# Expert stage of a routed kernel: weight loads coded per layer, one three-way branch per half of a unit, register loads in a unit's middle, the last scatter behind the late work

## The chip, the cores and the metric

The kernel runs on one core of one Trainium2 chip. The metric is the device time of one execution in microseconds (us), lower is better. The core has five engines with one instruction queue each: TensorE (PE; PEld is its weight load), VectorE (DVE), ScalarE (ACT), GpSimd (POOL) and SyncE (SP), which here issues the loads from HBM. A q behind an engine's name means its sequencer, which reads registers, takes branches and waits on semaphores.

## The reference, cut to what matters

An attention step and a dense layer are computed first. What the change touches is the third part, a mixture of experts over 2304 tokens of width 512, 8 experts, hidden width 1024:

```
expert_idx = np.argmax(logits, axis=1)
gate_w = probs[np.arange(N), expert_idx]
for e in range(E):
    mask = expert_idx == e
    h = np.maximum(x[mask] @ w1[e], 0.0)
    out[mask] = gate_w[mask, None] * (h @ w2[e])
```

w1[e] is 512x1024 and w2[e] is 1024x512, both in float32 (2 MB each).

## The kernel before, in words

The tokens are sorted by expert on the chip and cut into units of 256 places. A unit holds tokens of one expert. How many units there are, which expert each has and whether its second 128 places are filled is known only at run time, so it stands in an integer tile, `ctl` (row 0 the expert, row 1 a mode for the weights, row 2 the kind), and the engines read it into registers. In these data units U0 to U12 have work. Kind 2 is a double unit (both halves of 128), kind 0 a thin one (64 tokens at most, laid out so that the high and low parts share a matmul). Double are U0, U1, U2, U5, U6, U7, U10, U12; thin are U3, U4, U8, U9, U11.

A float32 product is made of three matmuls: high times high, high times low, low times high (`mm3`, L109 to L111). So weights are split after loading: ACT rounds a 128x1024 piece to a high part (L77), DVE subtracts for the low part (L78). There are two sets of split weights, one for even and one for odd units, and one staging set (tiles `sg`, `sq`, `sr` for w1, `sd`, `se` for w2). A unit needs new weights only where its expert differs from that of two units before: U3, U5, U6, U9, U10, U11.

The work stands in an order written by hand (`manual_schedule`), unit after unit. `gather` (POOL, L1016) fetches the rows of unit U+2; `group` makes the hidden values of a double unit, `grouped` their relu and split; `xt_turns` transposes the rows of the next unit, `xt_split` splits them, `fill` splits its weights from staging; `down` makes the output, `scale` (DVE) applies the gate and `scatter` (POOL, L1123) writes the rows out. A thin unit does the same in `single`, with its weights as the moving operand (L1141), 64 columns folded back by a matmul with `dots` (L1184). Where kind 1 would need the third product, a branch (L1145) takes either that product or as many matmuls with a zero tile `wz` (L1150, L1057).

For SP, `fetch(U)` stands behind unit U. It has three branches (L988), for units U+2, U+3 and U+4; the mode says which of them loads all of a unit's 4 MB (`fetch_all`: four DMAs of 512 KB for w1, L930, and four for w2, L933, each of these behind one of w1). The first DMA waits until staging is free, that is, until the last split of the earlier weights. `early_split` splits the weights of U0 and U1, which come in 256 KB pieces (`es`), ahead of this. `plan()` makes the tables: `counted`, `chain`, `placed` (the row lists, tile `perm`) and `listed` (`ctl`). Code for four further units (LATE, L1482) stands behind U12 and is jumped over.

Of the kernel before, what the change touches and what calls it, by code (L numbers as in the profile page):

```python
# [42 lines left out]
LATE = [range(U1, U1 + 2), range(U1 + 2, NU)]  # L43
SCALE = 1.0 / math.sqrt(D)
# [6 lines left out]
SOON = 400  # L51


def body(tc, x, state, w_in, w_out, ee, tau, w1, w2, out):
# [58 lines left out]
    with stack:  # L113
# [69 lines left out]
        def norm(ss, y, r, act=True):  # L183

            tsc(ss, ss, 1e-30, ALU.max)
            if act:
                A.activation(y, ss, AF.Ln)
                A.activation(y, y, AF.Exp, scale=0.5)
            else:
                G.tensor_tensor(out=y, in0=ss, in1=mb_[:, 3:4].to_broadcast(list(ss.shape)), op=ALU.pow)  # L190
            V.reciprocal(r, y)
# [435 lines left out]
        def route_n(c):  # L627
# [4 lines left out]
            norm(ssq[:, t0 : t0 + n], y, r, False)  # L632
# [62 lines left out]
        ctl = rt.tile([P, 3, NU], I32, name="ctl")  # L695
# [114 lines left out]
        def plan():  # L810
# [12 lines left out]
            def chain():  # L823
# [32 lines left out]
                oq = cut(NT, NX)  # L856
# [8 lines left out]
            def listed():  # L865
                cs, cx = held["cs"], held["cx"]
                kk, kb, gk, new = cut(NL), cut(NL), cut(NL), cut2(NU)
                V.memset(new[:, 0:U0], 1.0)
                c1, c2, c3 = (cut2(NL, NE) for _ in range(3))
# [13 lines left out]
                tsc(kk, new[:, 1 : NU - 1], 0.0, ALU.is_equal, -1.0, ALU.mult)  # L883
                tsc(gk, new[:, 0 : NU - 2], 0.0, ALU.is_equal, 1.0, ALU.add)
                tt(gk, gk, kk, ALU.mult)
                stt(ctl[:, 1, U0:NU], gk, 3.0, new[:, U0:NU], ALU.add, ALU.mult)
                tsc(ctl[:, 2, 0:1], n, float(U0), ALU.add)

                one, two = cut(NE), cut(NE)
# [8 lines left out]
                V.tensor_copy(ctl[:, 2, U0:NU], kk)  # L898

            return counted, chain, placed, listed  # L900
# [15 lines left out]
        staged, flag, mode = {}, {}, {}  # L916
        xg, gt_, xo, xth, xtl, hth, htl, hq, y_, ix_, ys_, hs_ = ({} for _ in range(12))
        FENG = [ET.Activation, ET.DVE]

# [9 lines left out]
        def fetch_all(e):  # L929
            one = [Y.dma_start(staged[1, i], w1[bass.ds(e, 1), i * P : (i + 1) * P, :].rearrange("o p f -> (o p) f")) for i in range(4)]  # L930
# [580 lines left out]
```

## Time and profile before

| | |
|---|---|
| median of 3 runs | 737.47 us (736.97 to 737.89) |
| the profiled execution | 734.5 us, its span 732.7 us |
| busy over the span | PE 93%, PEld 79%, DVE 65%, ACT 60%, POOL 25% |
| mean granted TensorE clock | 0.967 of full speed |
| expert stage (U0's first group to the end) | 425.36 to 732.7 us |

PE is busy for most of the span, so what can be won in the stage lies where its busy time is below the stretch's length, where its clock is below 1, or in work that needn't be there. The stage is cut at the starts of the units for this.

### The profile page before, as it was taken

The numbers are of one execution on the slowest core, as the hardware profiler recorded it, in microseconds if no ns is written. First come the engines' busy times: TensorE is split into PE (matmuls) and PEld (weight loads), VectorE is DVE, ScalarE is ACT, GpSimd is POOL, SyncE is SP. The second block draws the span as 40 slices with busy tenths as digits, with TensorE's granted clock in tenths as the row PEclk, the third lists the DMA queues.
The fourth block names the chain that finished last, engine by engine and source line by source line (L and its number), as shares of the span: only waits on it lengthen the run. The fifth ranks groups of instructions, "written<-read, shape, count | busy, mean of one in ns | idle before, by whom it ended". The sixth has DMA issues, their size and how long they took to land. (4 is left out here: it accounts for less than half of the span.)

```text
span 732.7 us, 12086 instructions
## 1 busy us (share of the span) xinstructions
PE 681.2 (93%) x3913; PEld 579.2 (79%) x3913; DVE 477.9 (65%) x1025; ACT 437.9 (60%) x771; POOL 183.7 (25%) x163
## 2 busy tenths in 40 slices
PE   8898999989999999999999999899888999859894
PEld 8898867768888888888878788888676997749593
DVE  5987898897587866766698778836273524543630
ACT  5877989988697768667867763225264212441510
POOL 2785356641000200300141420301310222101101
PEclk9899999999999999999999999999999999969898
DMA  8552243430010544411224452562834631427000
GB/s 200 152 154 87 59 144 114 144 116 0 1 58 14 143 104 100 93 40 58 73 58 138 151 173 58 174 234 86 294 109 188 236 112 61 164 100 263 32 2 33
DMA packets 58253, 82.84 MB, mean 113 GB/s; under 512 B 25051, under 2 KB 35803, under 8 KB 58149
## 3 DMA queue, kind: packets, MB, share of 16 engines
q1 hardware_dynamic: 54388, 70.31, 31.8%
q0 software_dynamic: 3760, 11.30, 4.6%
q8 instruction: 46, 0.75, 0.4%
q14 instruction: 59, 0.48, 0.2%
HBM read 65.32 MB, written 13.65 MB: 108 GB/s over the span
## 5 line engine op out<-in xcount | busy, mean ns | idle before, releaser
L109 PE MATMUL acc<-woh,gh 128*128 128x512 f32 x272 | 109.0, 404 | 4.9 <-ACT gh L77 4.9
L110 PE MATMUL acc<-wol,gh 128*128 128x512 f32 x272 | 107.7, 397 | 0.0
L111 PE MATMUL acc<-woh,gl 128*128 128x512 f32 x272 | 94.8, 402 | 0.5 <-DVE gl L78 0.5
L109 PE MATMUL hp<-xth,w1h 128*128 128x256 f32 x256 | 76.3, 298 | 9.8 <-ACT w1h L77 8.5
L111 PE MATMUL hp<-xth,w1l 128*128 128x256 f32 x256 | 76.5, 299 | 5.9 <-DVE w1l L78 5.3
L110 PE MATMUL hp<-xtl,w1h 128*128 128x256 f32 x256 | 75.0, 293 | 0.6 <-DVE xtl L78 0.6
L1123 POOL DMA_INDIRECT out<-ys,ix x21 | 21.6, 1029 | 212.3 <-DVE ix L1126 116.0
L109 PEld LDWEIGHTS acc<-woh,gh 128*128 128x128 f32 x272 | 51.2, 188 | 18.0 <-ACT gh L77 8.0
L111 PEld LDWEIGHTS acc<-woh,gl 128*128 128x128 f32 x272 | 51.2, 190 | 14.2 <-DVE gl L78 3.1
L518 ACT ACTIVATE er<-h,mb__104 128x512 f32<-128x512 f32 x68 | 46.6, 685 | 26.0 <-PE h L111 23.8
L109 PEld LDWEIGHTS hp<-xth,w1h 128*128 128x128 f32 x256 | 51.1, 200 | 11.3 <-ACT w1h L77 9.5
L110 PEld LDWEIGHTS acc<-wol,gh 128*128 128x128 f32 x272 | 51.4, 189 | 10.1
L1109 ACT ACTIVATE hth<-hp 128x512 fp32r<-128x512 f32 (+1 forms) x34 | 17.8, 532 | 67.5 <-PE hp L111 56.3
L111 PEld LDWEIGHTS hp<-xth,w1l 128*128 128x128 f32 x256 | 51.1, 199 | 8.6 <-DVE w1l L78 7.9
L524 DVE TENSOR_TENSOR er<-er 128x512 f32<-128x512 f32 x56 | 40.0, 715 | 21.6 <-ACT er L518 21.1
L547 ACT ACTIVATE h<-er,mb__104 128x512 f32<-128x512 f32 x68 | 47.3, 696 | 9.2 <-DVE er L524 5.6
L110 PEld LDWEIGHTS hp<-xtl,w1h 128*128 128x128 f32 x256 | 51.2, 200 | 1.1 <-DVE xtl L78 0.8
L109 PE MATMUL h<-xh,mh 128*128 128x512 f32 x128 | 51.6, 403 | 0.3 <-ACT xh L77 0.3
L110 PE MATMUL h<-xl,mh 128*128 128x512 f32 x128 | 50.7, 396 | 0.4 <-DVE xl L78 0.4
L111 PE MATMUL h<-xh,ml 128*128 128x512 f32 x128 | 50.6, 396 | 0.0
L548 ACT ACTIVATE er<-er,mb__104 128x512 f32<-128x512 f32 x68 | 49.4, 726 | 1.4
L519 ACT ACTIVATE u<-h 128x512 f32<-128x512 f32 x68 | 40.4, 594 | 0.0
(475 smaller groups left out, 1728.8 us busy)
## 6 DMA issues: line engine op xcount, KB each, us to landing
w<-in_moe_w_in SPq DMA_DIRECT2D x16, 512.0 KB
w<-in_moe_w_out SPq DMA_DIRECT2D x16, 512.0 KB
es<-in_moe_w SPq DMA_DIRECT2D x32, 256.0 KB
sg<-in_moe_w SPq DMA_DIRECT2D x12, 512.0 KB
sd<-in_moe_w SPq DMA_DIRECT2D x12, 512.0 KB
se<-in_moe_w SPq DMA_DIRECT2D x12, 512.0 KB
xn<-in_x SPq DMA_DIRECT2D x32, 128.0 KB
md<-mr SPq DMA_DIRECT2D x28, 128.0 KB
```

Of the source, the lines that this page charges most:

```text
L109: T.matmul(o, lh, rh, start=first, stop=False)
L110: T.matmul(o, lh, rl, start=False, stop=False)
L111: T.matmul(o, ll, rh, start=False, stop=last)
L518: A.activation(z, h, AF.Tanh, scale=0.5, bias=mb_[:, 0:1])
L519: A.activation(u, h, AF.Silu)
L524: V.tensor_tensor(out=z, in0=z, in1=z, op=ALU.mult)
L547: A.activation(r, z, AF.Square, scale=QS, bias=mb_[:, 1:2])
L548: behind["ACT"] = A.activation(z, z, AF.Square, scale=QS, bias=mb_[:, 2:3])
L1109: A.activation(hi, i, AF.Relu)
L1123: G.indirect_dma_start(out=out[:, :], out_offset=bass.IndirectOffsetOnAxis(ap=ix_[U][r], axis=0), in_=ys_[U][r], in_offset=None, bounds_ch ...
```

## The change

`plan()` makes one more table, `plan_` (in the unused part of `dots`): for each place behind a unit the expert whose w1 is to be loaded there, the one whose w2 is, or 8 for none, and for each unit a code `due_` of what is to be split in it. `listed` is cut into `experts`, `shapes` and `codes` and stands between the groups of U1. `fetch(U)` has two branches in place of three, and each loads one layer (`fetch_part`). With these data U3's weights are loaded behind U0, U5's behind U2, U6's w1 behind U3 and its w2 behind U4, U9's behind U5, U10's w1 behind U7 and its w2 behind U8, U11's behind U9. `fill(U)` splits what the next unit needs, `fill_soon(U)` the w1 of the unit after the next: U5's in U3 and U9's in U7, with only their w2 left for U4 and U8.

`either`, with its branches on `kp` and `kf` inside `single`, becomes `chosen`, a branch with three ways, taken once for the upper half of a unit (`up`) and once for the lower (`out_of`). Between the halves stands `next_rows`: the splits, and the register loads for units further on (`AHEAD`). The zero matmuls are gone, and both halves of the next rows are always transposed. Around U1 some pieces of `early_split` go to other places and four of them to POOL, U1's first group goes ahead of `placed`, and U1's `down` alternates between its two outputs. The scatter of U12's second half, from tiles of its own (`ixe`, `yse`), stands behind the LATE code.

```diff
+        def fetch_part(e, part):
             for i in range(4):
-                src = w2[bass.ds(e, 1), 2 * i * P : 2 * (i + 1) * P, :].rearrange("o (t p) d -> p (o t) d", p=P)
-                two = Y.dma_start(staged[2, i].rearrange("p (t d) -> p t d", t=2), src)
-                tc.add_manual_dep(two.ins, one[i].ins.name, mybir.DependencyInfo(mybir.DependencyClass.Sync, mybir.DependencyReason.DATA), reason="first layer first")
+                if part == 1:
+                    Y.dma_start(staged[1, i], w1[bass.ds(e, 1), i * P : (i + 1) * P, :].rearrange("o p f -> (o p) f"))
+                else:
+                    src = w2[bass.ds(e, 1), 2 * i * P : 2 * (i + 1) * P, :].rearrange("o (t p) d -> p (o t) d", p=P)
+                    Y.dma_start(staged[2, i].rearrange("p (t d) -> p t d", t=2), src)
...
-            for ahead in (1, 2, 3):
-                u = U + 1 + ahead
-                if u < U1:
-                    if u not in first:
-                        first[u] = expert(u, [ET.SP])
-                        mode[u] = nc.values_load(ctl[0:1, 1, u : u + 1], engines=[ET.SP], min_val=0, max_val=3)
-                    with tc.If(mode[u] == 4 - ahead):
-                        fetch_all(first[u])
+            for part in (1, 2):
+                cell = plan_[0:1, part, U : U + 1]
+                code = nc.values_load(cell, engines=[ET.SP], min_val=0, max_val=NE)
+                with tc.If(code < NE):
+                    fetch_part(nc.values_load(cell, engines=[ET.SP], min_val=0, max_val=NE - 1), part)
 
         def fill(U):
 
-            if U in flag:
-                with tc.If(flag[U] > 0):
-                    with tc.If(flag[U] > 1):
-                        split_all(U, [1])
-                    split_all(U, [2])
-            if U + 1 in flag and U > U0:
-                with tc.If(flag[U + 1] == 1):
+            with tc.If(due_[U] > 1):
+                with tc.If(due_[U] > 2):
                     split_all(U + 1, [1])
...
+                split_all(U + 1, [2])
+
+        def fill_soon(U):
+
+            with tc.If(due_[U] == 1):
+                split_all(U + 2, [1])
...
         def kinds(U):
 
-            for u in (U, U + 1):
-                if u < U1 and u not in flag:
-                    flag[u] = nc.values_load(ctl[0:1, 1, u : u + 1], engines=FENG, min_val=0, max_val=3)
-            kind[U], kp[U], kf[U] = (nc.values_load(ctl[0:1, 2, U : U + 1], engines=e, min_val=0, max_val=2) for e in ([ET.PE, ET.Pool] + FENG, [ET.PE], FENG))
+            cell = ctl[0:1, 1, U : U + 1]
+            kf[U] = nc.values_load(cell, engines=FENG, min_val=0, max_val=2)
+            kind[U] = nc.values_load(cell, engines=UENG, min_val=0, max_val=2)
+
+        def dues(U):
+            if U < END:
+                due_[U] = nc.values_load(plan_[0:1, 0, U : U + 1], engines=FENG, min_val=0, max_val=3)
...
         def xt_turns(U, parts=range(2)):
-            for i in parts:
-                for k in range(2 * i, 2 * i + 2):
-                    T.transpose(wide2(xo[U][i])[:, k % 2, 0:P], xg[U][0][:, k * P : (k + 1) * P], ident)
...
-            def second():
+            for r in range(2):
                 for i in parts:
                     for k in range(2 * i, 2 * i + 2):
-                        T.transpose(wide2(xo[U][i])[:, k % 2, P : 2 * P], xg[U][1][:, k * P : (k + 1) * P], ident)
...
-            with tc.If(kp[U] > 1) as w:
-                second()
-            with w.Else():
-                for k in range(2 * len(parts)):
-                    T.matmul(xo[U][1][:, 511:512], wz, wz[:, 0:1], start=True, stop=True, skip_group_check=True)
+                        T.transpose(wide2(xo[U][i])[:, k % 2, r * P : (r + 1) * P], xg[U][r][:, k * P : (k + 1) * P], ident)
...
-                with tc.If(kf[U] > 1) as w:
+                with tc.If(kf[U] > 0) as w:
...
+        def ends(U):
             ix_[U] = [rt.tile([P, 1], I32, tag="ix", bufs=2, name=f"ix{U}{r}") for r in range(2)]
             ys_[U] = [cv.tile([P, DM], F32, tag="cx", bufs=2, name=f"ys{U}{r}") for r in range(2)]
...
+            if U == END:
+                ix_[U][1] = rt.tile([P, 1], I32, name="ixe")
+                ys_[U][1] = ep.tile([P, DM + 2], F32, tag="xg", bufs=2, name="yse")[:, 0:DM]
...
-                scatter(U, r)
+                if U != END or not r:
+                    scatter(U, r)
...
+        def chosen(U, do):
+
+            with tc.If(kind[U] > 1) as w:
+                do(U, 2)
             with w.Else():
...
+                with tc.If(kind[U] > 0) as v:
+                    do(U, 1)
+                with v.Else():
+                    do(U, 0)
+
+        def up(U, n):
+            def rows_of_next():
+                if U + 1 in xo:
+                    xt_turns(U + 1)
+
+            if n > 1:
+                for j in range(4):
+                    group(U, j)
+                    grouped(U, j)
+                rows_of_next()
+                return
...
-
-            def turns(m):
-                with tc.If(kp[U] > 0) as w:
-                    for k in range(4):
-                        T.transpose(tr[m][:, k * P : (k + 1) * P], h[m][:, k * P : (k + 1) * P], ident)
...
-            if U + 1 < U1:
-                xt_turns(U + 1)
+            rows_of_next()
             turns(1)
             turned_(1)
-            following_rows(U)
...
+        def out_of(U, n):
+            if n > 1:
+                down(U)
+                store(U)
+                return
...
+        def next_rows(U):
+
+            if U < END:
+                xt_split(U + 1)
+                fill(U)
+            for u in AHEAD.get(U, ([], []))[0]:
+                kinds(u)
+            for u in AHEAD.get(U, ([], []))[1]:
+                dues(u)
+            if U + 2 <= END:
+                fill_soon(U)
...
-            early_split(2, V, G)
+            early_split(2, V)
...
+            early_split(2, V)
...
             group(0, 1)
+            early_split(3, V)
             squares(LC)
-            early_split(len(jobs) - 16, V, G)
...
-            early_split(2, V)
-            given = route_n(LC)
+            given = route_n(LC, lambda: early_split(3, V))
...
             grouped(0, 3)
+            xt_split(1)
+            early_split(4, G)
...
             down(0, [0], range(2, NFE))
-            down(0, [1], range(6))
+            down(0, [1])
+            ends(0)
+            for r in range(2):
+                scale(0, r)
+            rooms(1)
+            group(1, 0)
             placed()
             gather(2)
+            for r in range(2):
...
             tt(fold, ident[:, 0:HP], ident[:, HP:P], ALU.add)
-            down(0, [1], range(6, NFE))
-            store(0)
-            listed()
-            early_split(4, V)
-            rooms(1)
-            for j in range(4):
-                group(1, j)
-                grouped(1, j)
-                early_split(2, V)
...
+            grouped(1, 0)
+            group(1, 1)
+            experts()
+            grouped(1, 1)
+            early_split(2, V)
+            group(1, 2)
+            grouped(1, 2)
+            shapes()
+            group(1, 3)
+            grouped(1, 3)
+            codes()
             es_stack.close()
...
             stages()
             fetch(0)
-            for U in range(1, U1):
-                if U + 1 < U1:
-                    kinds(U + 1)
+            gather(3)
+            xt_tiles(2)
+            xt_turns(2)
+            kinds(2)
+            dues(1)
+            next_rows(1)
+            ends(1)
+            down(1, [(r, k) for k in range(NFE) for r in range(2)], None)
+            store(1)
+            fetch(1)
...
                 with cond(U):
-                    if U + 1 < U1:
+                    if U < END:
                         xt_tiles(U + 1)
-                    if U > 1:
-                        rooms(U)
-                    gather(U + 2)
-                    if U > 1:
-                        either(U)
+                    rooms(U)
+                    if U + 2 <= END:
+                        gather(U + 2)
+                    chosen(U, up)
+                    next_rows(U)
+                    if U < END:
+                        ends(U)
                     else:
-                        xt_turns(U + 1)
-                        following_rows(U)
-                        down(U)
-                        store(U)
-                fetch(U)
-
-            more = ExitStack()
+                        V.tensor_copy(ix_[U][1], gt_[U][1][:, 1:2])
+                    chosen(U, out_of)
+                if U + 2 <= END:
+                    fetch(U)
...
-                    either(U)
-            more.close()
+                    chosen(U, up)
+                    ends(U)
+                    chosen(U, out_of)
+            late.close()
+            scatter(END, 1)
```

On SP, the loads behind one unit. Before, this is the last of the three branches behind a unit (L988) with the reads for the next (L942 the expert, L987 the mode):

```order
L933 ISA
L933 DMA sd_5336<-in_moe_w 128x2x512
L933 ISA
L933 DMA se_5334<-in_moe_w 128x2x512
L933 ISA
L933 DMA se_5337<-in_moe_w 128x2x512
L988 UNCONDITIONAL_BRANCH x2
L942 TENSOR_LOAD ctl
L942 ISA x2
L987 TENSOR_LOAD ctl
L987 ISA x2
L988 COMPARE_AND_BRANCH
```

After, the two branches (L1026) for a layer each; a register is read from `plan_` (in `dots`) ahead of the branch and again inside it:

```order
L975 DMA se_5350<-in_moe_w 128x2x512
L1026 UNCONDITIONAL_BRANCH x2
L1025 TENSOR_LOAD dots
L1025 ISA x2
L1181 UNCONDITIONAL_BRANCH
L1091 UNCONDITIONAL_BRANCH
L1031 UNCONDITIONAL_BRANCH
L1038 UNCONDITIONAL_BRANCH
L1026 COMPARE_AND_BRANCH
L1027 TENSOR_LOAD dots
L1027 ISA x2
L972 ISA
```

The w1 DMAs (L972) and the w2 DMAs (L975) now stand in branches of their own, so one can be issued behind one unit and the other behind a later one, and no expert is read outside of the branch.

On PE, the middle of a thin unit. Before (L1057 is the last of the zero matmuls for the next rows, L1179 the branch on the kind, L1141 the output's matmuls):

```order
L1057 MATMUL gt_5697<-wz 128x1
L1057 LDWEIGHTS wz
L1057 MATMUL gt_5697<-wz 128x1
L1053 UNCONDITIONAL_BRANCH
L1187 UNCONDITIONAL_BRANCH
L1179 COMPARE_AND_BRANCH
L1181 MATMUL hp_5700<-ident,hs_5716 128x128 x4
L1179 UNCONDITIONAL_BRANCH
L1184 MATMUL hp_5700<-dots,hs_5716 128x64 x4
L1179 UNCONDITIONAL_BRANCH
L1141 MATMUL y_5703<-w2h_4601,hth_5705 128x512 x2
L1141 MATMUL y_5703<-w2h_4658,hth_5705 128x512 x2
```

After, the same place (L1081 the transposes of the next rows, L1212 the folding matmul, L1059 the register loads, L1181 the branch for the lower half):

```order
L1081 MATMUL gt_5648<-ident,xg_5404 128x128 x2
L1212 MATMUL hp_5651<-dots,hs_5663 128x64 x4
L1184 UNCONDITIONAL_BRANCH
L1059 TENSOR_LOAD ctl
L1059 ISA x2
L1059 TENSOR_LOAD ctl
L1059 ISA x2
L1091 UNCONDITIONAL_BRANCH
L1031 UNCONDITIONAL_BRANCH
L1038 UNCONDITIONAL_BRANCH
L1026 UNCONDITIONAL_BRANCH
L1181 COMPARE_AND_BRANCH
```

The branch ahead of the folding matmul is gone; behind it there are now the end of the three-way branch, the register loads, which stood at the unit's head before, and a new branch, whose thin side is reached by a jump over the double side and that of kind 1.

On POOL, the end. Before (L1123 the scatters of the last unit's second way, L1217 the end of its branch, L1482 the LATE branches):

```order
L1145 UNCONDITIONAL_BRANCH
L1210 UNCONDITIONAL_BRANCH
L1123 DMA out<-ys_12492,ix_12490 2176x512
L1217 ISA
L1217 UNCONDITIONAL_BRANCH
L1482 ISA
L1482 UNCONDITIONAL_BRANCH
L1482 ISA
L1482 UNCONDITIONAL_BRANCH
L1507 ISA
```

After (L1147 the scatters, L1546 the LATE branches):

```order
L1184 UNCONDITIONAL_BRANCH
L1147 DMA out<-ys_12311,ix_12309 2176x512
L1181 ISA
L1184 UNCONDITIONAL_BRANCH
L1546 ISA
L1546 UNCONDITIONAL_BRANCH
L1546 ISA
L1546 UNCONDITIONAL_BRANCH
L1147 DMA out<-yse,ixe 2176x512
L1572 UNCONDITIONAL_BRANCH
L1572 ISA
```

The last scatter, from `yse`, is now behind all the branches and behind the two ISA rows of L1546, which count POOL's DMA queue on.

## Rows read from the trace of the kernel before

**Rows 1.** By unit: length, PE, PEld, DVE, ACT, POOL busy, PEclk, DMA, GB/s
```profile
459.34:475.29 15.95, 14.00 (x98) 13.22 (x96) 12.62 (x43) 3.71 (x7) 6.95 (x6) 0.89 0.57 183
...
487.92:511.25 23.33, 23.33 (x153) 21.15 (x152) 11.99 (x16) 10.42 (x14) 2.97 (x3) 1.00 0.50 170
511.25:522.35 11.10, 10.91 (x74) 8.63 (x72) 4.46 (x14) 2.26 (x6) 1.02 (x1) 1.00 0.76 266
522.35:536.07 13.72, 11.63 (x73) 8.79 (x73) 4.99 (x10) 5.78 (x10) 6.39 (x6) 1.00 0.65 218
536.07:563.36 27.29, 25.37 (x158) 21.90 (x155) 13.70 (x19) 10.54 (x15) 2.93 (x3) 1.00 0.50 179
563.36:592.60 29.24, 25.94 (x153) 22.94 (x152) 15.68 (x23) 9.82 (x13) 5.00 (x5) 0.94 0.53 191
592.60:617.64 25.04, 23.47 (x153) 20.98 (x152) 10.22 (x17) 6.63 (x10) 4.50 (x5) 1.00 0.16 45
617.64:629.32 11.68, 10.96 (x72) 8.70 (x73) 4.12 (x9) 5.99 (x10) 2.46 (x3) 1.00 0.23 72
629.32:652.01 22.69, 12.70 (x72) 10.31 (x72) 6.80 (x12) 5.64 (x11) 2.94 (x3) 0.81 0.62 212
652.01:679.99 27.98, 27.89 (x153) 24.85 (x153) 14.35 (x21) 11.31 (x16) 2.94 (x3) 0.85 0.48 173
679.99:698.96 18.97, 15.46 (x74) 11.27 (x72) 11.77 (x18) 8.06 (x12) 2.02 (x2) 0.82 0.09 31
...
721.87:732.70 10.83, 0.01 (x1) 0.00 (x0) 0.75 (x1) 0.00 (x0) 0.98 (x1) 0.67 0.09 29
```

**Rows 2.** What PE waited for, 487 to 722: total, times, longest
```profile
PE hp L109 <- ACT w1h L77: 8.5, 1, 8.5
```

**Rows 3.** The same for SP's queue, and for ACT's splits, 480 to 733
```profile
SPq L930 <- DVEq L999: 69.0, 5, 34.0
...
ACT w1h L77 <- SPq L988: 28.5, 5, 9.6
```

**Rows 4.** SP's DMA issues, U10's weights: start, us, line, op
```profile
631.51 1.06 SPq L930 DMA_DIRECT2D sg<-in_moe_w  x2
...
638.26 2.27 SPq L933 DMA_DIRECT2D se<-in_moe_w  x2
```

**Rows 5.** PE in order of time, places in U4, U8 and U9
```profile
530.40 0.66 PE L1048 MATMUL gt<-ident,xg 128*128 128x128 f32 x4
...
628.36 0.35 PE L1150 MATMUL y<-wz 128*128 128x1 bf16 x8
...
652.01 0.58 PE L109 MATMUL hp<-xth,w1h 128*128 128x256 f32 x1 [8.45 <-ACT w1h L77]
```

**Rows 6.** PE's sequencer, branches of a line: ns min/median/max, first and last start
```profile
L1217 PEldq COMPARE_BRANCH  x19: 65/287/4006, 485.2 to 717.6; - x19
...
L1217 PEldq COMPARE_BRANCH  x1: 1052/1052/1052, 521.0 to 521.0; - x1
...
L1179 PEldq COMPARE_BRANCH  x10: 207/210/4690, 511.7 to 691.2; - x10
```

**Rows 7.** Splits and a small operation around U1, 400 to 480
```profile
L78 DVE TENSOR_TENSOR w2l<-es,w2h x11: 681/692/1685, 420.0 to 479.1; 128x512 fp32r<-128x512 f32 x11
...
L78 POOL TENSOR_TENSOR w2l<-es,w2h x4: 1286/1306/1610, 419.5 to 435.5; 128x512 fp32r<-128x512 f32 x4
...
463.43 0.23 DVE L64 TENSOR_SCALAR ph<-iof,ph 128x16 f32<-128x16 f32 x1
```

**Rows 8.** ACT and DVE in order of time, U5's first split of w1
```profile
533.72 2.01 ACT L77 ACTIVATE w1h<-sg 128x1024 fp32r<-128x1024 f32 x2 [0.30 <-SPq L988]
...
534.81 2.36 DVE L78 TENSOR_TENSOR w1l<-sg,w1h 128x1024 fp32r<-128x1024 f32 x2 [0.42 <-ACT w1h L77]
```

**Rows 9.** The end: POOL's last scatter, and its queue at the LATE branches
```profile
723.48 0.98 POOL L1123 DMA_INDIRECT out<-ys,ix  x1 [5.13 <-DMA out<-ys,ix]
...
L1482 POOLq INC_SWDGE_SEM  x1: 1105/1105/1105, 726.8 to 726.8; - x1
```

More of the change, by code (lines that the diff above doesn't have):

```diff
@@ L855, in chain @@
                 stt(g, g, 2.0, second, ALU.mult, ALU.add)
-                oq = cut(NT, NX)
+                oq = held["oq"] = cut(NT, NX)
                 tt(oq, row(iof[:, 0:NX], NT), col(g, NX), ALU.is_equal)
@@ L882, in listed, with shapes @@
                 tt(new[:, U0:NU], kk, gk, ALU.mult)
[L883 to L889, printed above, removed]
+                tsc(ctl[:, 1, 0:1], n, float(U0), ALU.add)
+            def shapes():
+                cs, one, two = held["cs"], cut(NE), cut(NE)
                 for w, blank in ((one, P), (two, P + P // 2)):
@@ L1131, in store, with high @@
                 scale(U, r)
-                scatter(U, r)
+                if U != END or not r:
+                    scatter(U, r)
         def lanes(t, half):
             return t.rearrange("p (k t) -> p k t", t=P)[:, :, half * HP : (half + 1) * HP]
-        def high(o, terms):
+        def high(o, terms, last):
             n = len(terms)
@@ L1140, in high, with low, sums @@
                 for k, (h, _, *w) in enumerate(terms):
[L1141 to L1143 removed]
+                    T.matmul(o, h, w[low], start=not low and k == 0, stop=last and bool(low) and k == n - 1)
+        def low(o, terms):
             n = len(terms)
[L1145 to L1167 removed]
+            for k, (_, l, wh, _) in enumerate(terms):
+                T.matmul(o, l, wh, start=False, stop=k == n - 1)
+        def sums(o, terms, thick):
+            high(o, terms, not thick)
+            if thick:
+                low(o, terms)
+        def chosen(U, do):
+            with tc.If(kind[U] > 1) as w:
+                do(U, 2)
+            with w.Else():
+                with tc.If(kind[U] > 0) as v:
[12 more added lines that the diff above has]
+                return
             q = U % 2
@@ L1214, in single, with cond @@
             scatter(U, 0)
-        def either(U):
-            with tc.If(kind[U] > 1) as w:
-                double(U)
-            with w.Else():
-                single(U)
+        def next_rows(U):
[8 more added lines that the diff above has]
+                fill_soon(U)
+        def cond(U):
+            return nullcontext() if U < UMIN else tc.If(nblk > U)
         steps = [(c, f) for c, a, b in RUNS for f in range(a, b)]
@@ L1425, in body @@
             places_of(range(CHUNKS[LC][0], NT))
-            counted, chain, placed, listed = plan()
+            counted, chain, placed, experts, shapes, codes = plan()
             down(0, [0], range(2))
@@ L1454, in body @@
+            kinds(2)
[5 more added lines that the diff above has]
+            fetch(1)
+            for U in range(2, U1):
+                if U == END:
+                    ends(U)
+                    V.memset(ix_[U][1], 2 * NTOK)
+                    V.memset(ys_[U][1], 0.0)
                 with cond(U):
-                    if U + 1 < U1:
+                    if U < END:
@@ L1472, in body @@
                 for U in g:
-                    gather(U, late=True)
+                    gather(U)
                     kinds(U)
-                    fetch_all(expert(U, [ET.SP]))
+                    e = expert(U, [ET.SP])
+                    for part in (1, 2):
+                        fetch_part(e, part)
                     split_all(U)
```

152 lines of the change are left out of this document (76 added, 76 removed).

## The prediction

> **What bounds the kernel now.** I read first the table of units [rows 1]: a unit's length against PE's busy time and PE's clock. U2 shows a double unit with nothing in its way: 23.33 us, PE busy for all of it, clock 1.00. U3 shows a thin one: 11.10 us. Held against these, the losses stand in a few rows: U5 is 27.29, U6 29.24, U7 25.04 and U10 27.98 against 23.3; U4 is 13.72, U9 22.69 and U11 18.97 against 11.1. Together these are 4.0 + 5.9 + 1.7 + 4.7 + 2.6 + 11.6 + 7.9 = 38.4 us, part idle PE, part PE at a lower clock (0.81 to 0.85 in U9 to U11). U1 has 1.95 us idle and a clock of 0.89.
>
> Then what PE waited for: one wait of 8.5 us, ahead of U10's first matmul, on ACT's split of its w1 [rows 2, 5]. Next, who was late for ACT: SP's branch, 28.5 us in 5 splits, 9.6 the longest [rows 3]. SP's branch is passed only when all eight loads have landed. And what was SP late for: it waited 69.0 us in 5 fetches for DVE's last split to free the staging, 34.0 us in one of them [rows 3]. So in U5 to U11 weights set the pace: one staging set, filled in one go and freed in one go. For U10 the loads were issued from 631.51, the last two at 638.26 to 640.53 [rows 4]; since a w2 load is issued only behind the landing of a w1 load, a layer takes about 640.5 − 631.5 = 9 us at most, two about 17, an estimate.
>
> The slow clock follows the idle time: U9's stretch, whose last 8.45 us are idle, has 0.81, and U10's busy time is 27.89 for the work that takes 23.33 in U2 [rows 1, 5].
>
> **The change, part by part.** The sum is made against the profiled execution: span 732.7, time 734.5 us, which is 3.0 below the median 737.47. The result is given at the median, so 3.0 is added at the end.
>
> *Loads per layer.* w1's staging is now free when w1 is split, and the new w1 can land while w2's staging is still full. U9's w1 is loaded behind U5 and split in U7, so U10's w1 can be asked for behind U7, not in the middle of U9. At U9's start (in the old times 629) it has had all of U8, 11.7 us, against the 9 of a layer: it has landed. Splitting it falls into U9's second half, as U5's did into U4's: there the split began at 533.72 and U5 began at 536.07 [rows 1, 8], which cost U5 27.29 − 23.33 = 4.0. I take this for U10: 27.3, so −0.7. U9 loses its wait and runs at full clock: 11.25, −11.4 (8.45 is the wait [rows 5], the rest clock and one late split). U11 then starts after an unbroken stretch: 11.4, −7.6. U5's w1 is split in U3, so U5 falls to 23.7, −3.6. U6 has its weights behind U3 and U4, with all of U5 for the split: 23.7, −5.5. U7, 25.04 with 23.47 busy: 24.3, −0.7. U8: 11.4, −0.3.
>
> Against this, U5's w1 split now stands on ACT and DVE around U4's start. Four pieces take about 4.2 us on ACT (2.01 for two) and 4.7 on DVE (2.36 for two) [rows 8], and U4's relu and split wait behind them in the queues, PE for these. Below, nothing (the pieces are done before U4 begins); above, the whole 4.7. U4's old stall was 13.72 − 11.63 = 2.1 [rows 1], and I take 14.5, +0.8.
>
> *Zero matmuls and transposes.* The eight behind a thin unit's output go (0.35 us in U8 [rows 5]), and two or three groups of four (half as many each); four transposes come wherever the next unit is thin, 0.66 us from the first start to the last end by U4's row [rows 5]; since matmuls overlap I take 0.4. U2 becomes 23.7 (+0.4). For thin units the two nearly cancel; U3 is set to 11.8 (+0.7), for the register loads now in its middle. If no engine's other work covers them there, they cost about 1 us in each of U3, U4 and U8; bounds 0 to 3 in all.
>
> *Around U1.* U1's idle 1.95 us goes if its w1 pieces are split earlier; part of its clock loss (15.95 × 0.11 = 1.75) with it. I take −2.4 from at most −3.7. The other bound is dearer: four pieces go to POOL, ahead of `chain`. A piece takes POOL 1.31 us, and DVE's like piece takes 0.69 us at the median but 1.69 at worst [rows 7]. Four times 1.31 = 5.2 us is what `chain`, and so U2's rows, can be later, which makes this term −2.4 to +2.8. [...] `codes` is about 21 small DVE operations at 0.23 [rows 7], 4.8 us behind U1's last group. U1's `down` covers them (24 matmuls for each half stand behind), and U3's weights, due only in U2's second half, cover SP's later start. Without the cover they'd cost the 4.8.
>
> *The last scatter.* Before, POOL's queue waited 5.13 us for the scatter before it, ended with that, issued at 723.48, 1.6 after PE's end at 721.87, and then counted its queue on for 1.1 us [rows 1, 9]. After, that count stands ahead of the scatter, hidden by U12's `down`. −1.0, between 0 and −1.6.
>
> *The sum.* Units: +0.4 +0.7 +0.8 −3.6 −5.5 −0.7 −0.3 −11.4 −0.7 −7.6 = −27.9. U1 −2.4, the end −1.0. New idle gaps (U4, U10) can pull the clock down again as in U9; for this +2, an estimate between none and the 4.6 that U10 paid. Together −29.3: the profiled execution would go to 705.2, the median to 708.2; I say **708.5 us**.
>
> **Rivals.**
>
> *Jumps (a).* Each thin unit now takes two long jumps on PE's sequencer, over the double side of each half, where it took one. The long branch of before (L1217) took 1.05 us at U4, 4.01 at its worst; its median over all units is 0.29, and the short branch L1179 took 0.21 at the median and 4.69 once [rows 6]. Why a branch takes 0.2 or 4 the rows don't tell. If the second jump stands on the path in all five thin units, this adds 5 × 1.05 to 5 × 4.01 = 5 to 20, middle 12.6, so about 721. For it speaks that nothing is queued on PE between the halves but the output, which waits for ACT and DVE anyway; against it, that this wait covers the cheap jumps, and that the halves are shorter than the whole that is jumped over now. Chance 0.17. [...]
>
> *Slower (b).* The same jumps with one more in each half: kind 0 is reached over the body of kind 2 and over that of kind 1. That is four taken branches in a thin unit, of which one was paid before. Two more exposed at the dear price, (4.01 + 4.69) / 2 = 4.35, on five units give 43.5, so 752. It ends above 737.5 from 29 / 5 = 5.8 us of new exposed branch time in each thin unit. The rows against it: of L1179's ten, the median is 0.21. Chance 0.05.
>
> *The loads come no earlier (c).* A layer's loads are still issued by one queue, and a branch not taken still waits for what landed before. If U10's w1 is held up so that it lands when it did, U9, U10 and U11 keep their length: 19.7 of the 29.3 are gone, 727.5. For it speaks the 34 us wait, which shows how one late split shifts everything; against it, that U9's w1 is split two units ahead. Chance 0.07.
>
> *More (d).* U4 and U10 have no stall, the clock stays up, U1's idle time and its clock loss go whole: −1.5, −4, −2, −1.3 and some of U7's 1: 699. Chance 0.07 for less than 699.
>
> **How the numbers follow.** The main case, 699 to 714 (U1's term alone reaches +5.2), has 0.64. Below 699 lie 0.07, between 714 and 724 (a) for the most part, above 724 the rest of (a), (c) and (b), about 0.15. The range is 697 to 724. A measurement of this kernel can tell about 0.2%, 1.5 us: only (b) and a part of what I don't see end above 739, so faster 0.93, same 0.01, slower 0.06.
>
> **What would show it.** In the profile after: no wait of PE for ACT of more than 4 us behind U4; U9 and U11 near 11.4 us at a clock near 1; SP's longest wait for DVE well under 34; U10's w1 issued about a unit earlier than U9's middle; U4 with a stall on ACT or DVE of 2 to 3 us. Wrong would be branches of PE's sequencer of over 2 us ahead of the lower halves with PE idle behind them (a, b), a PE wait ahead of U10 as before (c), or U2's start later than 487.9, which is where U1's part would have failed.

## The result, and the profile after

The changed kernel takes **704.29 us** (median of 4 runs, 698.74 to 705.4) against 737.22 in the runs beside it: ratio 0.955, 95% interval 0.9487 to 0.9614, or 33 us less. The forecast was 708.5, range 697 to 724. Six later runs gave 703.09 (700.22 to 707.35). The profiled execution, 698.74 us with a span of 696.9, is the fastest of its four, so its rows flatter the change: span against span it is 35.8 us, of which some 3 are not the usual case (U1 and the clock, below).

First the table of units again, of the changed kernel (length, then busy time of PE, PEld, DVE, ACT, POOL, then PE's clock, DMA share and GB/s). The first row is U1 up to its output, then come U2 to U11, and the end:

```profile
458.40:473.88 15.48, 13.02 (x122) 12.74 (x121) 14.72 (x52) 3.43 (x6) 6.42 (x6) 1.00 0.27 76
...
485.19:508.77 23.58, 23.58 (x154) 21.23 (x153) 13.48 (x20) 10.31 (x14) 4.00 (x4) 1.00 0.46 146
508.77:521.28 12.51, 10.45 (x58) 8.40 (x56) 4.80 (x12) 5.31 (x10) 4.45 (x4) 1.00 0.87 314
521.28:534.69 13.41, 10.54 (x56) 8.64 (x57) 7.71 (x14) 6.77 (x11) 3.11 (x4) 1.00 0.83 305
534.69:558.33 23.64, 23.64 (x154) 21.45 (x153) 18.10 (x22) 13.11 (x17) 2.94 (x3) 1.00 0.35 118
558.33:581.77 23.44, 23.44 (x153) 21.29 (x152) 6.60 (x15) 3.48 (x6) 5.00 (x5) 1.00 0.66 238
581.77:605.24 23.47, 23.47 (x154) 21.30 (x152) 9.47 (x16) 6.79 (x10) 4.01 (x4) 1.00 0.36 102
605.24:617.76 12.52, 10.47 (x58) 8.38 (x56) 5.18 (x10) 6.21 (x10) 2.98 (x3) 1.00 0.43 137
617.76:628.88 11.12, 10.68 (x57) 8.59 (x57) 6.97 (x13) 6.05 (x10) 2.95 (x3) 1.00 0.69 234
628.88:655.08 26.20, 24.51 (x153) 21.41 (x152) 21.50 (x26) 16.19 (x21) 2.95 (x3) 1.00 0.52 186
655.08:665.45 10.37, 10.33 (x57) 8.59 (x57) 3.97 (x11) 2.94 (x6) 2.01 (x2) 1.00 0.16 56
...
688.53:696.90 8.37, 0.00 (x1) 0.00 (x0) 0.75 (x1) 0.00 (x0) 0.98 (x1) 0.67 0.10 36
```

Against [rows 1], U5, U6 and U7 are now as long as PE is busy in them, with a clock of 1.00; U9 has gone from 22.69 to 11.12 and U11 from 18.97 to 10.37. U10 is the one double unit with a loss left, U3, U4 and U8 the thin ones. What PE and ACT still wait for, from U1 and from U2 on:

```profile
PE y L111 <- DVE ph L71: 2.5, 1, 2.5
PE hp L1167 <- issue: 2.4, 2, 1.4
PE hp L1167 <- ACT w1h L79: 2.0, 1, 2.0
...
PE hp L113 <- DVE w1l L80: 1.0, 2, 0.5
...
ACT w2h L79 <- SPq L1026: 0.6, 2, 0.3
```

The wait of 8.5 us [rows 2] has no successor, and of ACT's 28.5 us for SP's branch [rows 3] 0.6 are left. SP itself still waits for staging, in more and smaller pieces, and asks for U10's w1 in U7 (before, in U9 [rows 4]):

```profile
SPq L972 <- DVEq L1038: 44.3, 3, 18.1
...
SPq L972 <- DVE w1l L80: 22.7, 5, 21.0
```

```profile
598.69 1.47 SPq L972 DMA_DIRECT2D sg<-in_moe_w  x2
```

The clock differs from run to run (0.98 to 0.99 over the span). In the profile shown it never falls in the units; in a second profile of the same kernel (run again below, span 700.2) U1 and U4 read

```profile
459.70:488.70 29.00, 25.98 (x171) 23.09 (x170) 20.18 (x75) 4.51 (x8) 6.46 (x6) 0.94 0.43 126
524.90:538.20 13.30, 12.02 (x56) 9.79 (x57) 7.53 (x14) 6.58 (x11) 2.96 (x4) 0.87 0.84 302
```

which is a granted clock of 0.94 and 0.87 of full speed over the two, where PE was idle for 3.0 us in U1 and for 2.1 us right ahead of U4. U1 takes 29.0 us there for 26.8 in the profile shown. Another 2.9 us between the two profiles lie ahead of U0, in work that the change doesn't touch, where the clock is lower as well (0.95 and 0.98 in the first two stretches of 100 us, against 0.97 and 1.00).

### The profile page after: what moved, and what is told of

Its sections match the earlier page's. It is cut to its first block, busy times and chain, and to the rows that moved or that the text cites. A ratio compares the mean times of both kernels' runs of the same rounds, so it can differ in the third digit from the quotient of the medians.

```text
span 696.9 us, 11870 instructions
## 1 busy us (share of the span) xinstructions
PE 661.4 (95%) x3833; PEld 566.1 (81%) x3833; DVE 482.6 (69%) x1042; ACT 438.6 (63%) x771; POOL 184.4 (26%) x165
## 4 chain that ended last, share of the span: by engine, by line
PE 36%; DMA 27%; issue 12%; DVE 11%; ACT 9%; POOL 2%; SPq 2%; POOLq 0%; DVEq 0%; ACTq 0%
DMA out<-ys,ix 18%; PE acc L113 6%; PE acc L111 6%; PE acc L112 6%; DMA xg<-x1d,perm 4%; PE h L111 3%; PE h L112 3%; PE h L113 3%; DMA w<-in_moe_w_out 2%; SPq L329 2%; PE lg L628 2%; DMA w<-in_moe_w_in 1%; DMA es<-in_moe_w 1%; ACT er L522 1%; ACT h L551 1%
## 5 line engine op out<-in xcount | busy, mean ns | idle before, releaser
L113 PE MATMUL hp<-xth,w1l 128*128 128x256 f32 x256 | 72.5, 283 | 1.2 <-DVE w1l L80 1.0
L111 PE MATMUL hp<-xth,w1h 128*128 128x256 f32 x256 | 72.4, 283 | 0.5 <-DVE htl L74 0.5
L112 PE MATMUL hp<-xtl,w1h 128*128 128x256 f32 x256 | 72.2, 282 | 0.6 <-DVE xtl L80 0.6
L1147 POOL DMA_INDIRECT out<-ys,ix x20 | 20.2, 1008 | 171.7 <-DVE ix L1151 75.0
L113 PEld LDWEIGHTS hp<-xth,w1l 128*128 128x128 f32 x256 | 48.2, 188 | 1.8 <-DVE w1l L80 1.8
L111 PEld LDWEIGHTS hp<-xth,w1h 128*128 128x128 f32 x256 | 48.2, 188 | 1.2 <-DVE htl L74 0.7
L112 PEld LDWEIGHTS hp<-xtl,w1h 128*128 128x128 f32 x256 | 48.2, 188 | 1.2 <-DVE xtl L80 0.8
L111 PE MATMUL y<-w2h,hth 128*128 128x512 f32 x96 | 38.8, 404 | 2.6 <-DVE ph L71 2.5
```

Of the source, the lines that this page charges most:

```text
L111: T.matmul(o, lh, rh, start=first, stop=False)
L112: T.matmul(o, lh, rl, start=False, stop=False)
L113: T.matmul(o, ll, rh, start=False, stop=last)
L1147: G.indirect_dma_start(out=out[:, :], out_offset=bass.IndirectOffsetOnAxis(ap=ix_[U][r], axis=0), in_=ys_[U][r], in_offset=None, bounds_ch ...
```

## The experiments

Each was timed in 5 rounds. Ratios are to the kernel before; 0.01 is 7.4 us.

| run | what | median us | ratio (95%) |
|---|---|---|---|
| again | the change | 703.09 | 0.9578 (0.954 to 0.9616) |
| regs_head | register loads at the head | 703.65 | 0.9589 (0.9551 to 0.9626) |
| whole | that, and one branch for a unit | 716.78 | 0.9769 (0.9731 to 0.9807) |
| pad_up | code never run, in what is jumped over | 734.17 | 0.9972 (0.9942 to 1.0001) |
| joint | both layers loaded and split together | 711.94 | 0.9700 (0.9661 to 0.9739) |
| one_if | that, in one branch | 709.47 | 0.9627 (0.9586 to 0.9667) |
| idle_if | that, with a branch never taken behind | 725.16 | 0.9861 (0.9824 to 0.9898) |
| undo_all | whole and idle_if together | 739.57 | 1.0064 (1.004 to 1.0088) |
| last_back | last scatter in its old place | 704.76 | 0.9553 (0.951 to 0.9596) |
| split_v | four pieces on DVE, not POOL | 701.59 | 0.9546 (0.9526 to 0.9567) |
| shapes_early | table of kinds one group earlier | 699.55 | 0.9486 (0.9444 to 0.9528) |
| thin_first | that, with the thin way first | 706.33 | 0.9597 (0.9582 to 0.9613) |

**again.** No edit.

> The changed kernel unaltered, a second set of runs as the base for the others of this call: 704.3 again, between 699 and 709. If the spread of the first set (698.7 to 705.4) comes from TensorE's clock, a slower profiled execution has the same unit starts up to a place where the clock falls to half.

The time is as expected. The second profile, whose span is 3.3 us longer, is the one described above: it differs by the clock in U1 and U4 and ahead of U0, but also by 1.6 us in U0, which is the shorter there.

**joint.** No unit's w1 is asked for or split ahead of its w2:

```diff
-                V.memset(soon[:, 0 : U0 + 2], 0.0)
-                tt(soon[:, U0 + 2 : NU], new[:, U0 + 2 : NU], new[:, U0 + 1 : NU - 1], ALU.is_gt)
+                V.memset(soon[:, 0:NU], 0.0)
```

> Both layers of a unit's weights are asked for behind one unit and split in one unit, with all the rest of the change kept. If the timetable of the layers carries the gain, U10's weights are asked for only when U9's are split (in U8), land some 17 us later, and the wait ahead of U10 and the slow clock behind it are back: U5 +4, U6 +4, U9 and U10 +9, clock +4, so 725, and 718 to 732. If the shorter code in the units carries it (no zero matmuls, fewer branches, registers read in the middle), the time stays within 5 of the changed kernel: 704 to 709.

It lost 9 us, between the two expectations. U10's weights are asked for at 631.14, as late as before (631.51 [rows 4]), and yet U10 doesn't wait for them. Its w1 split begins 8.8 us after the request, without a wait (SP's request, then ACT, starts and busy times):

```profile
631.14 1.05 SPq L971 DMA_DIRECT2D sg<-in_moe_w  x2
...
639.02 1.08 ACT L79 ACTIVATE xth<-gt 128x512 fp32r<-128x512 f32 x2
639.97 2.02 ACT L79 ACTIVATE w1h<-sg 128x1024 fp32r<-128x1024 f32 x2
```

In the kernel before, the same split began 18.5 us after the request, and PE had 8.45 us of idle time behind it [rows 5]:

```profile
649.96 2.00 ACT L77 ACTIVATE w1h<-sg 128x1024 fp32r<-128x1024 f32 x2 [9.59 <-SPq L988]
```

Most of the loss that remains is U9's (6.7 us; U5 has some 3). In U9 DVE splits U9's own w2 until 630.94; U8's gate stands behind this on DVE and ACT, and ACT's copy of U9's hidden values (633.10) behind that; PE waits 4.93 us there and the clock falls:

```profile
633.75 0.47 PE L1211 MATMUL hp<-dots,hs 128*128 128x64 f32 x1 [4.93 <-ACT hs L1221]
```

```profile
624.80:642.60 17.80, 12.83 (x56) 10.63 (x57) 11.51 (x17) 9.60 (x14) 2.94 (x3) 0.81 0.57 191
```

So something other than the earlier request had removed the long wait.

**one_if.** On top of joint, one branch for all eight loads:

```diff
-            for part in (1, 2):
-                cell = plan_[0:1, part, U : U + 1]
...
-                with tc.If(code < NE):
-                    fetch_part(nc.values_load(cell, engines=[ET.SP], min_val=0, max_val=NE - 1), part)
+            with tc.If(code < NE):
+                e = nc.values_load(cell, engines=[ET.SP], min_val=0, max_val=NE - 1)
+                for part in (1, 2):
+                    fetch_part(e, part)
```

> As the kernel with joint loads (711.9, which asks for U10's weights at 631.1, when the kernel before did), with one change: the eight loads stand in one branch on SP, not four in each of two. If a separate branch is what lets ACT split w1 while w2 is still landing (U10's w1 split began at 640.0 with joint loads and at 650.0 in the kernel before), the waits of 8 to 10 us ahead of U6, U10 and U11 are back: 720 to 732. If only the time of asking matters, it equals the joint loads: 710 to 714.

My theory fell: no wait came back, and the time is rather below joint's than above it. ACT's split of U10's w1, asked for at 628.16 with w2 in the same branch, doesn't wait at all:

```profile
636.16 1.07 ACT L79 ACTIVATE w1h<-sg 128x1024 fp32r<-128x1024 f32 x1
```

**idle_if.** On top of one_if, a branch that is never taken behind the loads, since the kernel before had two more candidate branches there:

```diff
+            with tc.If(code > NE):
+                e = nc.values_load(cell, engines=[ET.SP], min_val=0, max_val=NE - 1)
+                for part in (1, 2):
+                    fetch_part(e, part)
```

> As one_if (709.5, both layers in one branch), with a second branch behind it on SP that could load the same tiles and is never taken, as two of the three branches were in the kernel before. Theory: such a branch has to wait for the landings before it lets ACT go on, and this, not the number of loads in the taken branch, is what held ACT's split of w1 to w2's landing (SP's queue in the kernel before: the branch is passed at 640.76, its semaphores at 647.81, ACT's split at 649.96). Then the waits of 8 to 10 us ahead of U6, U10 and U11 are back: 722 to 735. [...]

It lost 16 us more, and the old waits are back at U6, U10 and U11:

```profile
565.12 2.01 ACT L79 ACTIVATE w1h<-sg 128x1024 fp32r<-128x1024 f32 x2 [7.62 <-SPq L1028]
651.69 2.00 ACT L79 ACTIVATE w1h<-sg 128x1024 fp32r<-128x1024 f32 x2 [8.63 <-SPq L1028]
...
678.54 2.01 ACT L79 ACTIVATE w1h<-sg 128x1024 fp32r<-128x1024 f32 x2 [7.77 <-SPq L1028]
```

U9 and U10 read as they did before [rows 1], with the slow clock behind the idle time:

```profile
628.20:652.80 24.60, 12.78 (x57) 10.35 (x57) 9.75 (x16) 7.95 (x13) 2.95 (x3) 0.76 0.57 194
652.80:681.50 28.70, 27.86 (x152) 24.32 (x153) 15.70 (x21) 12.79 (x18) 2.95 (x3) 0.85 0.46 169
```

On SP's queue the branch behind U10's loads is passed at 640.17, its first semaphore operation starts at 640.34, the last packet of the loads ends at 650.97, the next semaphore operation starts at 651.48 and ACT's split at 651.69. (In one_if the packets go on until 643.81, and ACT's split began at 636.16.) SP's waits there (total, times, longest):

```profile
SPq L1028 <- SPq L1028: 62.3, 9, 11.1
```

So in this kernel a branch that writes the same tiles and is not taken waits for the loads in flight before it lets the readers go on, and the readers wait for it. The change has no second branch for the same layer behind the taken one until the next unit's place.

**regs_head** and **whole.** First the reads alone go back to a unit's head, then in addition one branch holds a whole unit:

```diff
+                    registers(U)
                     if U < END:
                         xt_tiles(U + 1)
                     rooms(U)
```

> The register loads go back to the head of a unit, ahead of its rooms and gather; all else as changed. They take about 0.5 us a unit on PE and 0.5 to 1.3 us on ACT and DVE. If they're hidden in either place, no difference that can be told (within 1.5 us). If the head is the exposed place, as the prediction of U4's stall in the kernel before has it, 1 to 4 us longer.

No difference. Then whole:

```diff
-                    chosen(U, up)
-                    next_rows(U)
...
-                    chosen(U, out_of)
+                    def all_of(U, n):
+                        up(U, n)
+                        next_rows(U)
+                        out_of(U, n)
+
+                    chosen(U, all_of)
```

> One three-way branch for a whole unit, with the next rows and the splits inside each way, and the register loads at the head: the code has one long jump in a thin unit in place of two, but a longer one. If jumps on PE's sequencer cost (rival a), it is faster than the kernel with the loads at the head, by the exposed part of five jumps, 2 to 10 us. If the jumps are hidden, within 2 us of it. If a longer jump is dearer (the 4.44 us branch ahead of U4 in the changed kernel, 2.0 of it seen by PE), 2 to 8 us slower.

It lost 13 us, more than the last guess. The jump over the longer ways is dear nearly each time. On PE's sequencer, the branches of the second way (ns, min/median/max):

```profile
L1184 PEldq COMPARE_BRANCH  x7: 179/3010/5234, 510.1 to 678.1; - x7
```
PE's first matmul of U3 and of U8, with the idle time ahead of it:

```profile
513.78 0.47 PE L1167 MATMUL hp<-w1h,xth 128*128 128x512 f32 x1 [3.31 <-issue]
...
617.90 0.77 PE L1167 MATMUL hp<-w1h,xth 128*128 128x512 f32 x1 [6.26 <-issue]
```

In the changed kernel the same branches are cheap, all but two of the first kind (4.44 us ahead of U4, 3.04 ahead of U11). The rows of them all, and PE's wait behind the one ahead of U4, which ends at 520.72:

```profile
L1181 PEldq COMPARE_BRANCH  x34: 65/184/4441, 481.0 to 684.2; - x34
...
L1184 PEldq COMPARE_BRANCH  x12: 181/212/293, 505.2 to 662.6; - x12
```

```profile
521.28 0.47 PE L1167 MATMUL hp<-w1h,xth 128*128 128x512 f32 x1 [2.02 <-ACT w1h L79]
```

**pad_up.** Length alone, with no change in what is executed (kind 1 doesn't occur in these data):

```diff
                 sums(hq[U][m], terms(m), n)
+                if n:
+                    for _ in range(64):
+                        T.matmul(hq[U][m][:, 0:1], wz, wz[:, 0:1], start=True, stop=True)
```

> The changed kernel with 128 zero matmuls added to the way of kind 1 in the upper half, which these data never take: the work that is executed is the same, and only the code that is jumped over is longer. If the length of a jump sets its price, the branch to a thin unit's upper half (0.2 us in all but two of ten) takes 3 to 5 us in most of the five thin units, as in the kernel with one branch for a whole unit, and 5 to 13 us are lost. If the price comes from something else, 703 as before.

It lost some 30 us, nearly the whole gain and more than twice the highest guess. The branch that took 0.21 us, on the sequencer, and then the other one:

```profile
L1184 PEldq COMPARE_BRANCH  x10: 207/1620/6005, 512.6 to 688.3; - x10
...
L1181 PEldq COMPARE_BRANCH  x29: 65/219/6132, 486.6 to 685.1; - x29
```

Double units pay too, since they leave their way over the two others: the 6.13 us are U10's, between its upper half and its lower one. PE waits ahead of the output as well as ahead of a unit (total, times, longest):

```profile
PE hp L1167 <- DVE ys L66: 5.8, 1, 5.8
PE hp L1167 <- issue: 5.7, 2, 3.1
PE y L111 <- ACT w1h L79: 5.5, 2, 4.0
PE y L111 <- DVE w1l L80: 4.2, 1, 4.2
PE y L111 <- ACTq L1038: 3.3, 1, 3.3
```

The names behind the arrows are what ended nearest. That a branch was the cause is read from the sequencer: the wait of 5.8 us ends at 532.35, and a branch of 5.74 us began at 526.28 and ended at 532.02.

What such a branch waits for stands in the trace too, among the DMA packets. From 526.28 to 532.02 the queue whose kind is "instruction" brings one packet of 16 KB, which has landed at 530.62 (packets, MB, share):

```profile
q8 instruction: 1, 0.02, 1.1%
```

From 500 us on, PE's sequencer has eleven branches of over 2.5 us in pad_up, and each ends 1.3 to 1.6 us after such a packet has landed. The changed kernel has three, the one at the LATE code included, and they end 1.4 to 1.5 us after one. So a dear branch waits for code to be loaded, and with the longer way this happens eleven times in place of three.

**undo_all.** The edits of whole and idle_if in one kernel.

> One branch for a whole unit, register loads at the head, both layers asked for and split together, and the never-taken branch behind the loads; without the zero matmuls, with the table made in U1 and the last scatter behind the late code. If these are the causes and they add up, it takes as long as the kernel before, 730 to 742; what it falls short of it is what the zero matmuls, the end and U1 are worth, at most 5.

739.57, ratio 1.0064, within the range. From the parts one gets 0.9861 + (0.9769 − 0.9589) = 1.0041: they add up. It comes out 0.6% above the kernel before, not below it. So what is left of the change (no zero matmuls, the transposes of both halves, w2 loads that no longer wait for w1's, U1, the end, and a three-way branch for a two-way one) saves nothing in sum here; what each of these is worth the runs don't separate.

**last_back.** `scatter(END, 1)` back into `store`, with the shared tiles.

```diff
-            scatter(END, 1)
...
-                if U != END or not r:
-                    scatter(U, r)
+                scatter(U, r)
```

> The last scatter goes back into U12's lower half, ahead of the late code, with the shared tiles; all else as changed. The prediction's term for it is 1.0 (0 to 1.6): so 1 us longer than the changed kernel, and 2.5 if the whole difference of the ends after PE's last matmul (10.8 before, 8.4 after) is its doing. No difference if the change of the end comes from elsewhere.

The time doesn't tell the two apart. In the profile the stretch behind PE's end is 10.27 us against 8.37, so about 1.9 us, but not for my reason (below).

**split_v.** `early_split(4, G)` becomes `early_split(4, V)`.

> The four pieces of w2 that the change splits on POOL are split on DVE instead; all else as changed (703.5). Prediction's term: POOL's pieces can hold DVE up for as much as 5.2 us, and PE waits 0.4 to 3.1 us for DVE in U0's output in the changed kernels, nowhere there before. If POOL's splits are what holds DVE up, that wait goes and U1 begins 1 to 3 us earlier. If they relieve DVE, whose own four pieces take 2.8 us, U1 begins later by up to 2.8 us.

Ratio 0.9546 against 0.9578, with intervals that overlap: POOL's pieces bring nothing that shows. The wait for DVE in U0's output is absent here, but it is also only 0.17 us in the second profile of the changed kernel (1.73 in the first). What it costs stays open.

**shapes_early.** `shapes()` moves up to stand right behind `experts()`.

> The table of kinds is made right after that of experts, one group of U1 earlier. In the changed kernel PE waits 2.5 to 3.0 us ahead of U1's output; its sequencer reads U2's and U3's kinds there, and the read waits for that table. If that is the wait, it goes or shrinks to under 1 us, and the time falls by 1.5 to 3 us. If PE waits there for the relu of U1's last group (DVE has it done 0.5 us earlier), it stays.

It is the fastest kernel of all, 699.55, some 0.9% or 4 to 7 us under the change. In the changed kernel DVE writes the table, and PE waits 2.47 us ahead of U1's output:

```profile
472.16 0.27 DVE L901 CAST ctl<-ph 128x16 int32<-128x16 f32 x1
...
473.88 0.49 PE L111 MATMUL y<-w2h,hth 128*128 128x512 f32 x1 [2.47 <-DVE ph L71]
```

Between the two stand the reads on PE's sequencer, at 472.5 and 473.2 (ns, min/median/max):

```profile
L1059 PEldq TENSOR_LOAD <-ctl x2: 303/311/319, 472.5 to 473.2; - x2
```

With the earlier table, in shapes_early, 0.52 us are left:

```profile
474.83 0.49 PE L111 MATMUL y<-w2h,hth 128*128 128x512 f32 x1 [0.52 <-issue]
```

The clock didn't fall there either, so it gets back twice: U1 is 24.80 us against 29.00, with a clock of 0.94, in the second profile of the change (26.8 in the first, where the clock didn't fall):

```profile
461.30:486.10 24.80, 24.28 (x170) 21.87 (x169) 19.99 (x74) 4.52 (x8) 6.65 (x6) 1.00 0.33 102
```

**thin_first.** On top of shapes_early, the order of the ways:

```diff
-            with tc.If(kind[U] > 1) as w:
-                do(U, 2)
+            with tc.If(kind[U] < 1) as w:
+                do(U, 0)
```

> shapes_early (699.6) with the way of kind 0 first in the code of each half, then kind 2, then kind 1: a thin unit enters a half without a jump and leaves it over the two others; a double one jumps over the short way. If the long jump costs because it stands ahead of a unit's first matmul, where PE has little queued, the wait ahead of U4 (2.0 us) goes: 696 to 699. If leaving over the same distance costs the same, or costs more since it stands between the halves, 699 to 706.

706.33, so 7 us worse. The wait ahead of U4 is gone, but the jump is now behind the upper half, where PE has nothing queued, and the output of U3 waits:

```profile
520.36 0.76 PE L1167 MATMUL y<-w2h,hth 128*128 128x512 f32 x1 [4.53 <-ACT w1h L79]
```

The name behind the arrow isn't the cause: the relu that this matmul needs was done at 516.7. PE's sequencer shows nothing from 515.05, behind the register loads, to the lower half's branch at 520.11, and a packet of code lands at 518.47. In U8 the jump itself is the dear one, with 3.41 us of idle time on PE:

```profile
L1181 PEldq COMPARE_BRANCH  x4: 68/137/4210, 615.7 to 621.5; - x4
```

## Why the prediction was right

Forecast 708.5, measured 704.3, and the sum of units from U2 to U12 (U12 as before) was 206.0 against 203.3 in the profile. Point by point:

- *Weights set the pace.* Right. Asking for them per layer is worth about 9 us (joint), the branches without an idle one behind them 16 (idle_if against one_if). But my sum puts nearly the whole gain down to the weights, and idle_if, which undoes both, is still 11 us below the kernel before (725.16 against 736.16). With one branch for a unit as well (undo_all) nothing is left. I had no term for the shorter ways, and part of what I gave to the weights is theirs.
- *"U10's w1 can be asked for behind U7 ... U9 loses its wait ... −11.4".* The size was right (U9 11.12 for 11.25), the reason half wrong. joint asks for U10's w1 as late as before and has no wait of 8 us. It was the never-taken branch that held ACT up. I named it, in rival (c), only as a thing that could stay in the way, and didn't see that the coded cell takes it away; the same for U6 and U11. "SP's branch is passed only when all eight loads have landed" was a wrong reading too: in one_if eight loads stand in the taken branch, and ACT's split of w1 doesn't wait.
- *U5, U6, U7.* 23.64, 23.44, 23.47 for 23.7, 23.7, 24.3. *U10* 26.20 for 27.3, with PE idle for 1.7 of it, most in two waits of 0.5 us for w1l and one for the relu.
- *U4's split stall.* 13.41 for 14.5. U3 is 12.51 for 11.8, but with a cause that I gave no share in the main case: 2.02 us behind the branch of 4.44 us, which is rival (a). U8 is 12.52 for 11.4, with PE idle for 1.06 ahead of its output, for a relu on DVE, and for 0.99 ahead of U9.
- *U1, −2.4.* This step failed. U1 to U2's start took 28.6 us before (459.34 to 487.92 [rows 1]) and 28.9 to 29.1 in three profiles with it (again, regs_head, last_back; 26.8 in the one shown above). In the second profile of the change U2 starts at 488.7, which is my sign of this failure. I put the idle time for w1l down as saved and overlooked what the change adds: PE reads kinds between U1's hidden values and its output, and has to wait for the table. shapes_early shows what the term could have been, about −4. Of the other bound of this term, 5.2 us of delay by POOL's four pieces, no run shows the whole: beside them DVE takes 2.96 us for four operations on `Q` in the profile shown (446.99; 0.88 before, at 448.15) and 1.23 for one on `ph` (449.87; 0.17 before, at 448.95), so 3.1 us more, and split_v, where DVE has the four, is at 0.9546 against 0.9578.
- *The end, −1.0.* 8.37 for 10.83, so −2.5. The count on POOL's queue was not hidden: it ran at 688.67, behind PE's end, and the scatter went out 2.35 us after PE's end (1.6 before). What is saved lies behind it: POOL's closing drain starts at 690.7 and lasts 5.37 us beside the landing, where in last_back the landing (2.56), the count (1.1) and a drain of 3.91 follow one another. The scatter in the changed kernel:

```profile
690.88 0.98 POOL L1147 DMA_INDIRECT out<-yse,ixe  x1 [5.91 <-issue]
```

POOL's drains there, and then those of last_back (ns, first and last start):

```profile
L1572 POOLq DRAIN  x3: 46/113/5369, 690.7 to 696.6; - x3
```

```profile
L1560 POOLq DRAIN  x3: 46/107/3913, 699.3 to 703.7; - x3
```

- *The clock, +2.* Nothing in the profile shown; in the second profile of the change two falls, in U1 and U4, of 1.7 us each (0.06 of 29.0 and 0.13 of 13.3).
- *Rival (c), 0.07.* Its sum is 708.2 + 19.7 = 727.9, not 727.5. idle_if, where a branch not taken does hold the weights up, took 725.16.
- *Rival (a), 0.17, and (b), 0.05.* Two dear branches in the units, one of them seen by PE. But pad_up shows that the length of what is jumped over decides, and that 128 matmuls more in a way that is never taken would have put the time at 734. The forecast rested on "the halves are shorter than the whole that is jumped over now", which whole and pad_up bear out, and I had not worked out how near the edge that is: so far it was luck. L1184's branches, 0.21 us at the median in the changed kernel, take 1.62 in pad_up and 3.01 in whole. Why in the changed kernel it is U4's and U11's jumps that wait for code, and not U3's, U8's or U9's, no run shows.

That the total came within 4.2 us is in part luck as well: U1's 2.4, which didn't come, and the excess of U3 (0.7) and U8 (1.1) were made up by U4 and U10 (1.1 each) and by the end (1.5).

## What to carry to other kernels

Where code is chosen at run time, look at what is jumped over and not only at what is run: split long ways into short ones (one branch for a whole unit lost 13 us here, 128 matmuls never run some 30), and put a jump where the engine has work queued (7 us in thin_first). A conditional load that wasn't taken still waited here for the one that was, and everything that reads the tile waited with it (16 us); one load with a coded operand did better than several candidates. When a read of a register goes to another place, look at which table it waits for there (2.47 us of PE in U1).

## What the runs showed of the hardware that I had not expected

Code that is never executed cost some 30 us: the same branch of PE's sequencer took 0.21 us at the median, 1.62 with 128 matmuls added to the way that it passes over, and up to 6.0. Each of the eleven longest there ends 1.3 to 1.6 us after a 16 KB packet of code has landed. And an idle time of 2 to 3 us on PE can cost nearly as much again by a lower granted clock: 1.7 us each in U1 (3.0 us idle, clock 0.94) and in U4 (2.1 us ahead of it, clock 0.87) in the second profile of the change, none with waits of 2.5 and 2.0 us in the first, where both units have 1.00. In the kernel before the clock is 0.50 from 652 to 660, behind the wait of 8.45 us.
